# Top-k attention and a GELU MLP: the first batch's attention tile row by tile row, its MLP in chunks of 128 tokens

## The chip, the cores and the metric

The kernel runs on one core of a Trainium2 chip. The core has a matrix engine (PE, with PEld for its weight loads), a vector engine (DVE), an activation engine (ACT), a general engine (POOL), and queues that issue DMAs (SP's above all). The metric is the device time of one execution in microseconds (us), the median of several runs; lower is better.

## The reference

Inputs are q, k, v of 8 batches, 8 heads, 576 tokens, 64 columns, and two weight matrices, 512 x 2048 and 2048 x 512, which arrive in double precision.

```python
scores = scale * np.matmul(q, k.transpose(0, 1, 3, 2))
kth = np.partition(scores, -32, axis=-1)[..., -32:-31]
scores = np.where(scores >= kth, scores, -1000000000.0)
attn = np.exp(scores - np.max(scores, axis=-1, keepdims=True))
attn = attn / (np.sum(attn, axis=-1, keepdims=True) + 1e-09)
x = np.matmul(attn, v)                    # then (B,H,S,D) -> (B*S, H*D) = 4608 x 512
h = x @ w_in
g = 0.5 * h * (1.0 + erf(h / sqrt(2)))
return g @ w_out
```

## The kernel before

**Attention.** Heads are taken in pairs: 4 pairs a batch, 32 in all. An item is a pair and a tile of 128 query rows (`t` 0 to 3); the last 64 rows of two pairs make one item (`t` = 4). There are 18 items a batch, 144 in all, and the list `items` gives their order. One slot `n` of the main loop runs, for different items at once: `scores(n + 2)` (PE, copied to SBUF by ACT), the search `top_k(n)` on DVE, `threshold(n)` on POOL, the two `softmax(n - 1, e)` halves on ACT (they leave the unnormalised P and its row sum `den`), `add_small` (POOL) and `inverse` (DVE, `rden` = 1/den), `normalise(n - 1)` (POOL: P times `rden`, 128 x 1152), `transposes(n - 2)` (PE, copied to `pt` by ACT) and `attend(n - 3)` (PE: P times v for two tiles of a pair at once, 256 columns wide, copied to `xT` by ACT).

A search finds the 32nd largest of 576 scores by rounds of eight (MAX8, then MATCH_REPLACE8). A paired search works on lists of 288, the larger and the smaller of two halves (`larger` on DVE, `sum_up` and `smaller` on POOL); a single search (items below `PAIRED` = 2, and those in `SINGLE`, 18 to 27) works on all 576.

**Weights.** 16 units of two 128 x 512 blocks come as double-precision words and are turned to float32 in three steps (`weights_size`: two on ACT, the third on ACT or, for slots in `ON_DVE`, on DVE) and an addition on POOL (`weights_add`), one unit a slot from slot 1 on in `ORDER`. A unit's words are loaded two slots ahead into buffers that lie in weight arrays not yet filled.

**MLP.** x is kept transposed in `xT`. The tokens are cut in `units` of a token range and some of the 16 row blocks `f` of `w_in`; pairs of units make blocks of eight pieces. First-layer pieces (`l1_piece`) are products of `w_in` with 256 (or 128) tokens. GELUs run on ACT when a block is done. Second-layer pieces are plain for the first 256 tokens (`full_piece`, 512 wide) and, for the tokens after them, seven products in place of eight (`seven_piece`, `trio_piece`; they need POOL's `sums` of g and, made once in slots `sums_in`, `weight_sums` of `w_out`), or for a tail of 128 tokens `even_piece`. All blocks stand in one list `pieces`. `mlp(n)` runs the next n of them at places in the slot, within `room_in(slot)`: four in slots 10 and 11, then one block a slot, one piece more or less by turns. Nothing runs before the first 256 tokens of all four pairs are done, that is before slot 10 (`ready`). Until then `keep_busy` gives PE products of the identity.

PSUM has eight banks: two for scores and transposes (`pr`), two for first-layer blocks (`l1`), three for the second layer (`y0` to `y2`), and `z`. Small PE results (`bank`) turn through `z`, `y0`, `y1`, `y2` until `few` is set in slot 13, and then use `z` alone.

The order on each engine is the order in which the program issues; each engine waits in order.

## Time and profile before

| | us |
|---|---|
| median of 3 runs (1557.78 to 1558.49) | 1557.83 |
| the profiled execution, first to last instruction (its span) | 1553.6 |
| PE busy | 1524.1 |
| DVE busy | 1330.3 |
| ACT busy | 1166.7 |
| POOL busy | 1141.6 |
| start of slot 0 (first MAX8 of the search) | 10.29 |
| start of slot 30 | 316.84 |

The span stands for the execution's own time; the median is 4.2 us above it. Rows that name a line of the kernel give the engine, the operation, what it writes and reads, its shape and count; then the busy time in us, the mean length of one instruction in ns, and the idle time of the engine before them, with who ended it. An instruction's mean length contains what overlaps with the next one. Rows of stretches give the stretch, its length, and per engine the busy time and the number of instructions, then PE's granted clock, the DMA engines' busy share and GB/s. Rows of the timeline and the merged chain start with the time in us and the length.

### The profile page before, as it was taken

The numbers are of one execution on the slowest core, as the hardware profiler recorded it, in microseconds if no ns is written. First come the engines' busy times: TensorE is split into PE (matmuls) and PEld (weight loads), VectorE is DVE, ScalarE is ACT, GpSimd is POOL, SyncE is SP. The second block draws the span as 40 slices with busy tenths as digits, with TensorE's granted clock in tenths as the row PEclk, the third lists the DMA queues.
The fourth block names the chain that finished last, engine by engine and source line by source line (L and its number), as shares of the span: only waits on it lengthen the run. The fifth ranks groups of instructions, "written<-read, shape, count | busy, mean of one in ns | idle before, by whom it ended". The sixth has DMA issues, their size and how long they took to land.

```text
span 1553.6 us, 28121 instructions
## 1 busy us (share of the span) xinstructions
PE 1524.1 (98%) x9280; PEld 1199.8 (77%) x9280; DVE 1330.3 (86%) x4571; ACT 1166.7 (75%) x2050; POOL 1141.6 (73%) x1291
## 2 busy tenths in 40 slices
PE   8999999999999999999999999999999999999998
PEld 6776578877777778887777778788777777787887
DVE  7998799999989988898989998988998998998700
ACT  6998887777777787777777777777777777777720
POOL 4986657767787868777787877776788786876632
PEclk9999999999999999999999999999999999999999
DMA  6513210012101110012201111012110111000000
GB/s 176 164 67 128 70 45 1 1 41 50 24 15 31 38 28 27 1 30 45 40 15 18 28 31 45 1 24 36 32 24 22 24 30 32 15 1 15 7 14 14
DMA packets 185297, 56.35 MB, mean 36 GB/s; under 512 B 176160, under 2 KB 176704, under 8 KB 185152
## 3 DMA queue, kind: packets, MB, share of 16 engines
q1 hardware_dynamic: 183888, 54.13, 14.6%
q8 instruction: 73, 1.20, 0.3%
q14 instruction: 72, 0.59, 0.1%
q10 hardware_dynamic: 1200, 0.39, 0.1%
q0 software_dynamic: 64, 0.03, 0.0%
HBM read 45.08 MB, written 9.44 MB: 35 GB/s over the span
## 4 chain that ended last, share of the span: by engine, by line
PE 79%; POOL 6%; DVE 3%; ACT 1%; issue 1%; DVEq 0%; POOLq 0%
PE h_ps L668 29%; PE y_ps L806 17%; PE o L610 8%; PE tp L553 7%; PE s_ps L370 6%; PE seven L804 3%; POOL s L507 2%; PE y_ps L768 2%; PE y_ps L771 2%; PE tp_t L333 2%; PE o L621 1%; PE y_ps L750 1%; PE tp_t L527 1%; PE s_ps L385 1%; DVE top L450 1%; DVE lists L453 1%
## 5 line engine op out<-in xcount | busy, mean ns | idle before, releaser
L668 PE MATMUL h_ps<-xT,w_in_sb 128*128 128x256 f32 (+1 forms) x2560 | 542.7, 361 | 1.9 <-ACT xT L615 1.9
L668 PEld LDWEIGHTS h_ps<-xT,w_in_sb 128*128 128x128 f32 x2560 | 433.7, 191 | 72.6 <-issue 25.3
L450 DVE MAX8 top<-lists 128x8 f32<-128x288 f32 x792 | 321.2, 447 | 0.0
L507 POOL TENSOR_TENSOR s<-s,rden 128x1152 f32<-128x1152 f32 x144 | 302.7, 2102 | 0.3 <-DVE rden L482 0.3
L496 ACT ACTIVATE s<-s,bias 128x576 f32<-128x576 f32 x288 | 223.4, 776 | 11.9
L453 DVE MATCH_REPLACE8 lists<-top,lists 128x288 f32<-128x288 f32 x528 | 229.8, 443 | 0.0
L495 ACT ACTIVATE s<-s,neg 128x576 f32<-128x576 f32 x288 | 225.8, 784 | 2.9 <-POOL neg L475 2.7
L450 DVE MAX8 low<-lists 128x8 f32<-128x288 f32 x528 | 213.1, 446 | 0.0
L569 ACT COPY pt<-tp 128x1024 f32<-128x1024 f32 x133 | 135.1, 1016 | 102.0 <-PE tp L553 102.0
L488 POOL TENSOR_SCALAR den<-den 128x2 f32<-128x2 f32 x144 | 31.4, 218 | 233.4 <-ACT s L496 229.0
L421 POOL TENSOR_TENSOR lists<-lists 128x576 int32<-128x576 int32 x132 | 186.3, 1411 | 4.0
L413 POOL TENSOR_TENSOR lists<-s 128x576 int32<-128x576 int32 x132 | 185.6, 1406 | 0.0
L610 PE MATMUL o<-pt,raw_v 128*64 128x256 f32 x1280 | 153.4, 385 | 0.4 <-ACT pt L560 0.4
L610 PEld LDWEIGHTS o<-pt,raw_v 128*64 128x64 f32 x1280 | 86.6, 137 | 86.6 <-issue 44.1
L475 POOL TENSOR_SCALAR neg<-kth 128x2 f32<-128x2 f32 x132 | 85.7, 649 | 88.6 <-DVE kth L466 88.0
L553 PE MATMUL tp<-ident,s 128*128 128x128 f32 x1152 | 149.6, 273 | 0.0
L553 PEld LDWEIGHTS tp<-ident,s 128*128 128x128 f32 x1152 | 134.6, 141 | 14.8 <-issue 1.6
L806 PE MATMUL y_ps<-w_out_sb,sum 128*128 128x256 f32 x480 | 142.8, 379 | 0.0
L482 DVE RECIPROCAL rden<-den 128x2 f32<-128x2 f32 x144 | 23.3, 162 | 136.9 <-POOL den L488 136.2
L378 ACT ACTIVATE s<-s_ps 128x1024 f32<-128x1024 f32 x127 | 124.2, 1025 | 15.7 <-PE s_ps L370 15.4
L370 PE MATMUL s_ps<-kt,qm 64*128 64x512 f32 x512 | 131.4, 627 | 0.8 <-ACT s L376 0.8
L684 ACT ACTIVATE g<-h_ps 128x512 f32<-128x512 f32 x144 | 78.2, 595 | 49.9 <-PE h_ps L668 49.2
(148 smaller groups left out, 2826.4 us busy)
## 6 DMA issues: line engine op xcount, KB each, us to landing
raw_v<-in_v_dram SPq DMA_DIRECT2D x64, 128.0 KB, 2.3
out_dram<-y SPq DMA_DIRECT2D x30, 256.0 KB, 2.1
w_out_sb<-in_moe_w_in_dram SPq DMA_DIRECT2D x14, 511.8 KB, 4.9
raw_q<-in_q_dram SPq DMA_DIRECT2D x96, 64.0 KB, 2.0
raw_k<-in_k_dram SPq DMA_DIRECT2D x96, 64.0 KB, 2.0
w_out_sb<-in_moe_w_out_dram SPq DMA_DIRECT2D x10, 511.8 KB, 4.2
w_sum<-in_moe_w_out_dram SPq DMA_DIRECT2D x6, 511.8 KB, 4.0
raw_q<-in_q_dram SPq DMA_DIRECT2D x96, 8.0 KB, 1.8
```

Of the source, the lines that this page charges most:

```text
L370: nc.tensor.matmul(s_ps[:, e], lhsT=q_t[rows, :], rhs=kt[rows, 0:SM], start=True, stop=True)
L413: nc.gpsimd.tensor_tensor(t[:, 1].bitcast(i32), a.bitcast(i32), b.bitcast(i32), op=ALU.add)
L421: nc.gpsimd.tensor_tensor(both, both, top, op=ALU.subtract)
L450: nc.vector.max(x[:, e], src[:, e])
L453: nc.vector.match_replace(dst[:, e], x[:, e], src[:, e], LOWEST)
L495: nc.scalar.activation(s, s, func=AF.Prelu, bias=st["neg"][:, e : e + 1], scale=1.0, alpha=STEEP)
L496: nc.scalar.activation(s, s, func=AF.Exp, bias=st["bias"][:, e : e + 1], scale=1.0, accum_out=st["den"][:, e : e + 1],)
L507: nc.gpsimd.tensor_tensor(s, s, wide, op=ALU.mult)
L553: nc.tensor.transpose(tp[:, j * P : (j + 1) * P], s[:, first + j * P : first + (j + 1) * P], ident)
L610: nc.tensor.matmul(o[e * D : (e + 1) * D, 0:n], lhsT=vt[:, j, e, :], rhs=pt[:, e * NM + j if j < NM else 2 * NM, :], start=(j == 0), stop= ...
L668: nc.tensor.matmul(h_tile(u)[:, i, :], lhsT=w_in_sb[:, ko, f * P : (f + 1) * P], rhs=xT[:, ko, c0 : c0 + n], start=(ko == 0), stop=(ko == ...
L806: nc.tensor.matmul(acc[names][:, k], lhsT=lhsT, rhs=rhs, start=(j == 0 and k == 0), stop=(j == FT // 2 - 1 and k == 1),)
```

## The change

- The first batch's 16 whole-tile items come tile by tile and, within one, pair by pair: `items` for b = 0 is `(p, t)` with t outermost. After four items 128 tokens are done for all pairs. The raw q and k of all four pairs are loaded and transposed ahead, three pairs before slot 0, on three queues.
- These items run in `early_slot`: transposes in the slot of their softmax (`n - 1`), `attend(n - 2)` for one tile, 128 columns wide. P isn't normalised; two products with a broadcast `rden` put 1/den in the same bank, ACT copies the product to `xT`, and DVE multiplies it there, behind round 0 of the slot's search.
- The first 640 tokens of the MLP are plain; the first 512 of them in chunks of 128. Blocks of the first two chunks are interleaved; two first-layer blocks (`HELD`) stand in `y0`, `y1`. The MLP begins in slot 5, and from slot 12 to 29 its pieces are spread evenly; from slot 30 on a slot has the blocks that it had before.
- Units are converted in the order 0 to 15 in slots 1 to 16; the third step runs on DVE for slots 8 to 16. Single searches move to slots 31 to 39, `weight_sums` to 30 to 37.
- Small PE results turn through `z` and `y2` from slot 5 to 17.

```diff
@@ raw q and k
+    front = w_sum.rearrange("p a b n -> p (a b n)")
+    for y, region in enumerate((early, front[:, 0 : 2 * RAW], front[:, 2 * RAW : 4 * RAW])):
+        for x, n in enumerate("kq"):
+            raws[n].append(region[:, x * RAW : (x + 1) * RAW].rearrange("p (j e d) -> p j e d", j=NJ, e=2))
...
-    ORDER = [0, 1, 2, 3, 8, 9, 4, 5, 10, 11, 6, 7, 12, 13, 14, 15]
+    ORDER = list(range(UNITS))
     START = 2 * NP + 2
+    FIRST = NP + 1
+    EARLY = NP * NM
-    ON_DVE = range(START + 1, START + 9)
-    SINGLE = range(18, 28)
+    ON_DVE = range(8, UNITS + 1)
+    SINGLE = range(31, 40)
-    SLOT_OF = dict(zip(ORDER, [*range(1, START + 1), *range(START + 3, START + 9)]))
+    SLOT_OF = dict(zip(ORDER, range(1, UNITS + 1)))
...
         main = [
             (b * NP + p, tt + d) for tt in range(0, NM, 2) for p in range(NP) for d in range(2)
-        ]
+        ] if b else [(p, t) for t in range(NM) for p in range(NP)]
...
-        tag = "z" if few[0] else ("z", "y0", "y1", "y2")[turn[0] % 4]
+        tags = ("z",) if few[0] else ("z", "y2") if begun[0] else ("z", "y0", "y1", "y2")
+        tag = tags[turn[0] % len(tags)]
...
@@ top_k
             if r == len(rounds) - 1:
                 last()
+            if r == 0:
+                yield
@@ normalise
-        if i < 0 or i >= N:
+        if i < EARLY or i >= N:
             return
@@ transposes
+        if i < EARLY:
+            new_pt()
+            pr[0] = pair_tile("tp")
+            def ends():
+                nc.scalar.copy(
+                    out=pt_now[0][:, 0 : 2 * NM, x : x + P],
+                    in_=pr[0].rearrange("p e (j n) -> p (e j) n", j=NM),
+                )
+                tails(None)
+            return [lambda: turn_over(pr[0][:, 0], 0), lambda: turn_over(pr[0][:, 1], 1), ends]
@@ attend
-            copies.append(lambda: nc.scalar.copy(out=xT[:, at, c], in_=o[:, 0:n]))
+            if i < EARLY:
+                r = stat_of[i]["rden"]
+                for e in range(2):
+                    wide = bass.AP(
+                        tensor=r.tensor, offset=r[:, e : e + 1].offset, ap=[list(r.ap[0]), [0, D]]
+                    )
+                    nc.tensor.matmul(
+                        o[e * D : (e + 1) * D, P : 2 * P], lhsT=wide, rhs=ident, start=True, stop=True
+                    )
+                nc.scalar.copy(out=xT[:, at, c], in_=o[:, 0:P])
+                copies.append(lambda: nc.vector.tensor_tensor(
+                    xT[:, at, c], xT[:, at, c], o[:, P : 2 * P], op=ALU.mult
+                ))
...
@@ units
-        for tok, n in ((0, 256), (256, 256), (SM, 2 * TL), (COLS, 256), (COLS + 256, 256)):
+        whole = [(0, 256), (256, 256)] if base else [(t * P, P) for t in range(NM)]
+        for tok, n in (*whole, (SM, 2 * TL), (COLS, 256), (COLS + 256, 256)):
...
+    HELD = (2, 6)
...
-        return "even" if n < 256 else "full" if tok == 0 else None
+        return "full" if tok < COLS else "even" if n < 256 else None
...
-    blocks = [behind(first_block(0), 7, 0), behind(first_block(2), 7, 2)]
-    for u in range(2, NU, 2):
+    blocks = [behind(first_block(u), 7, u) if u in HELD else first_block(u) for u in (0, 2, 4, 6)]
+    blocks += [second_block(0), second_block(4), behind(first_block(8), 7, 8)]
+    blocks += [second_block(2), second_block(6), behind(first_block(10), 7, 10)]
+    for u in range(10, NU, 2):
         blocks.append(second_block(u - 2))
...
+    SPREAD = (12, 30)
     def room_in(n):
         x = n - START - 1
-        if x < 1:
-            return 4
+        if n < SPREAD[0]:
+            return min(7 if n < 9 else 6, sum(sizes[:4]) - done[0])
+        if n < SPREAD[1]:
+            ends = sum(sizes[:4]), sum(sizes[: SPREAD[1] - START - 1])
+            part = (n - SPREAD[0] + 1) / (SPREAD[1] - SPREAD[0])
+            return min(10, round(ends[0] + part * (ends[1] - ends[0])) - done[0])
         if x >= len(sizes):
             return 0
         return sizes[x] + (1 if x % 2 == 0 else -1)
...
-    load("k", 1)
+    load("k", 1, nc.scalar)
     load("q", 1)
-    for n in range(1, 3):
-        load_weights(n)
+    load("q", 2)
+    load("k", 2, nc.scalar)
+    load("k", 3, nc.gpsimd)
+    load_weights(1)
+    load("q", 3)
+    load("v", 0)
+    load_weights(2)
...
-    sums_in = {START + 8 + j: j for j in range(FT // 2)}
+    sums_in = {30 + j: j for j in range(FT // 2)}
+    def early_slot(n):
+        left[0] = room_in(n) if n >= FIRST else 0
+        begun[0] = n >= FIRST
+        if not waits(unit_in(n)):
+            weights_add(unit_in(n))
+        larger(n + 1)
+        scores(n + 2)
+        product = attend(n - 2)
+        searches = top_k(n, lambda: inverse(n - 1))
+        next(searches)
+        copy_x()
+        ready[0] = n_tok[0]
+        softmax(n - 1, 0)
+        mlp(1)
+        softmax(n - 1, 1)
+        if waits(unit_in(n)):
+            weights_size(unit_in(n))
+            weights_add(unit_in(n))
+        u = unit_in(n + 1)
+        whole = u is None or waits(u)
+        if not whole:
+            weights_size(u, 0)
+        mlp(2)
+        if n < FIRST:
+            keep_busy(6 if product else 12, ident)
+        prep = prep_in.pop(n, [])
+        for piece in prep[:1]:
+            piece(None)
+        tr = transposes(n - 1) if n - 1 < EARLY else []
+        for piece in tr:
+            piece()
+            mlp(1)
+        for piece in prep[1:]:
+            piece(None)
+            mlp(1)
+        if n < FIRST:
+            keep_busy(8, ident)
+        smaller(n + 1)
+        add_small(n - 1)
+        mlp(left[0])
+        if not whole:
+            weights_size(u, 1)
+        run_gelus()
+        for _ in searches:
+            pass
+        threshold(n)
+        normalise(n - 1)
+        sum_up(n + 2)
+        run_small(6)
+        next_loads(n)
+    LAST_EARLY = EARLY + 1
+    for n in range(LAST_EARLY + 1):
+        early_slot(n)
     ahead = N + 4
-    for n in range(ahead):
+    for n in range(LAST_EARLY + 1, ahead):
...
-        two = few[0] and n % 2 == 0 and n + 3 < N and items[n + 3][1] < NM
+        two = n % 2 == 0 and n + 3 < N and items[n + 3][1] < NM and not h_of
```

More of the change, by code (lines that the diff above doesn't have):

```diff
@@ L295, in piece @@
             ahead = 1 if pair >= SQUARES else 2
-            if pair + ahead > SQUARES and pair < SQUARES and pair % 2:
+            if pair < NP or pair + ahead > SQUARES and pair < SQUARES and pair % 2:
                 return
@@ L909, in first_block, with words_of @@
         need = units[u][0] + units[u][1]
-        return [(need, lambda w=w, x=x: l1_piece(w, x)) for w in (u, u + 1) for x in range(4)]
+        def words_of(w, x):
+            _, _, f0, nf = units[w]
+            c = 2 * ((f0 + x // (4 // nf)) * P // WS)
+            return (c, c + 1)
+        return [
+            (need, words_of(w, x), lambda w=w, x=x: l1_piece(w, x)) for w in (u, u + 1) for x in range(4)
+        ]
     def second_block(u):
@@ L955, in mlp @@
         for _ in range(n):
-            if done[0] >= len(pieces) or pieces[done[0]][0] > ready[0] or left[0] == 0:
+            if done[0] >= len(pieces) or pieces[done[0]][0] > ready[0] or left[0] <= 0:
                 return
-            pieces[done[0]][1]()
+            if not all(w in made for w in pieces[done[0]][1]):
+                return
+            pieces[done[0]][2]()
             done[0] += 1
@@ L992 @@
     keep_busy(WARM, idle)
-    for pair in range(2):
+    for pair in range(3):
         for piece in transpose_qk(pair, pair == 0):
             piece()
-        if pair == 0:
-            scores(0)
-            scores(1)
+        if pair < 2:
+            scores(pair)
     slots_of = [
@@ L1011 @@
     ]
-    first = {2: (0, 1, 1), 3: (2, 2, 3)}
+    first = {3: (0, 0, 0)}
     prep_in, squares_in = {}, {}
-    for pair in range(2, n_pairs):
+    for pair in range(3, n_pairs):
         b, p = divmod(pair, NP)
@@ L1089 @@
         ready[0] = n_tok[0]
-        if late:
-            softmax(n - 1, 1)
+        softmax(n - 1, 1)
         smaller(n + 1)
         add_small(n - 1)
-        for piece in tr[-1:] + prep:
+        for piece in prep[1:]:
             piece(None)
             mlp(1)
-        if n == 1:
-            keep_busy(8, ident)
         run_gelus()
@@ L1103 @@
         if n < N:
-            top_k(n, lambda: inverse(n - 1))
+            for _ in top_k(n, lambda: inverse(n - 1)):
+                pass
         else:
@@ L1112 @@
         run_small(6)
-        if not waits(unit_in(n + 1)):
-            weights_size(unit_in(n + 1))
-        for m in (n + 1, n + 2):
-            if m > 2 and waits(unit_in(m)) == (m == n + 1):
-                load_weights(m)
-        if n < NP:
-            load("v", n)
     ready[0], left[0] = NT, len(pieces)
```

138 lines of the change are left out of this document (72 added, 66 removed).

## The prediction

> **What bounds the kernel now.** I read the page first, then the busy time of each engine in stretches cut at the starts of attention slots, then single slots in the timeline, then the groups by form for prices.
>
> ```profile
> span 1553.6 us, 28121 instructions
> PE 1524.1 (98%) x9280; PEld 1199.8 (77%) x9280; DVE 1330.3 (86%) x4571; ACT 1166.7 (75%) x2050; POOL 1141.6 (73%) x1291
> PE   8999999999999999999999999999999999999998
> DVE  7998799999989988898989998988998998998700
> ```
>
> PE looks full from start to end. It isn't, as the prices of its groups show:
>
> ```profile
> L668 PE MATMUL h_ps<-xT,w_in_sb 128*128 128x256 f32 x2048 | 480.8, 382 | 1.9 <-ACT xT L615 1.9
> L610 PE MATMUL o<-pt,raw_v 128*64 128x256 f32 x1280 | 153.4, 385 | 0.4 <-ACT pt L560 0.4
> L668 PE MATMUL h_ps<-xT,w_in_sb 128*128 128x128 f32 x512 | 61.9, 277 | 0.0
> L990 PE MATMUL warm<-ident 128*128 128x128 f32 x366 | 46.6, 287 | 0.0
> L750 PE MATMUL y_ps<-w_out_sb,g 128*128 128x512 f32 x64 | 29.8, 592 | 0.0
> ...
> L668 PEld LDWEIGHTS h_ps<-xT,w_in_sb 128*128 128x128 f32 x2560 | 433.7, 191 | 72.6 <-issue 25.3
> ```
>
> L990, 46.6 us, multiplies the identity for nothing. All of it lies in the first ten slots, where the MLP has no input yet. The stretches below are slots 0 to 4, 5 to 10, 11 to 17, 18 to 29, 30 to 39, 40 to 143, and what follows the last search (columns: length, then busy time and instructions of PE, PEld, DVE, ACT, POOL, clock, DMA share, GB/s):
>
> ```profile
> 10.29:57.68 47.39, 39.11 (x244) 28.45 (x244) 47.28 (x139) 41.21 (x69) 31.41 (x28) 0.89 0.69 196
> 57.68:112.31 54.63, 52.61 (x411) 43.65 (x410) 53.12 (x193) 53.75 (x90) 49.31 (x43) 1.00 0.24 86
> 112.31:192.37 80.06, 77.47 (x407) 47.63 (x407) 64.25 (x230) 70.38 (x113) 51.54 (x46) 1.00 0.34 102
> 192.37:316.84 124.47, 123.94 (x854) 98.18 (x853) 118.39 (x280) 97.55 (x172) 86.40 (x116) 1.00 0.08 21
> 316.84:416.78 99.94, 98.97 (x548) 78.43 (x546) 92.93 (x331) 76.83 (x138) 71.64 (x79) 1.00 0.20 36
> 416.78:1470.90 1054.12, 1047.65 (x6432) 831.74 (x6429) 949.17 (x3387) 808.53 (x1438) 819.89 (x933) 1.00 0.12 24
> 1470.90:1553.60 82.70, 76.16 (x362) 65.18 (x360) 2.85 (x8) 15.97 (x34) 28.88 (x40) 0.98 0.04 13
> ```
>
> Call them A, B, C, D, E, F, G. In A and B the search on DVE sets the pace (47.28 of 47.39, 53.12 of 54.63). In C it is PE together with the softmax chain, in D PE and DVE together, from E on PE with DVE close behind. One slot's cost on DVE stands in the timeline, paired and single searches:
>
> ```profile
> 48.81 0.45 DVE L450 MAX8 first<-lists 128x8 f32<-128x288 f32 x1
> 57.68 0.46 DVE L450 MAX8 first<-lists 128x8 f32<-128x288 f32 x1
> ...
> 244.88 0.74 DVE L450 MAX8 first<-s 128x8 f32<-128x576 f32 x1
> 254.58 0.74 DVE L450 MAX8 first<-s 128x8 f32<-128x576 f32 x1
> ```
>
> A paired search takes 8.87 us a slot, a single one 9.70: 0.83 more.
>
> **The sum, stage by stage.** The list of MLP blocks has the same length from slot 30 on, so each slot there gets the same pieces as before. F and G I leave at their times. What changes is how long it takes to reach slot 30, and E. All terms are against the profiled execution of 1553.6 us, which lies 4.2 us below the median of 1557.83; I add the sum to the median.
>
> Prices of a piece, from the merged chain (16 wide, 32 narrow instructions, 24 of the seven-product blocks):
>
> ```profile
> 646.97 3.57 PE h_ps L668 x32
> ...
> 1474.27 3.46 PE h_ps L668 x16
> ...
> 1507.98 5.18 PE y_ps L806 x24
> ```
>
> A 256-wide instruction takes 0.216 us, a 128-wide one 0.112. A first-layer piece is 4 x 0.216 = 0.86 before and 8 x 0.112 = 0.89 after: 64 pieces of the first 512 tokens cost 1.9 us more in all. The Trainium skill, "TensorE: Matmul & The Clock Gate", section "Back-to-back issue gap", speaks against narrow chunks: in a stream with weight loads it gives about 81 ns a matmul at N=128 and 131 at N=512, far from proportional; halfway (an estimate, 98 ns at 256) a narrow pair would cost 1.65 times the wide one, and the 64 pieces about 36 us more instead of 1.9. The rows here, 3.57/32 against 3.46/16, disagree with it.
>
> A second-layer piece is two 512-wide instructions, 2 x 29.8/64 = 0.93 us. A seven-product block is 28 instructions of 0.216, 6.0 us; eight plain pieces are 7.4.
>
> A, slots 0 to 4. Three products of xT by the broadcast reciprocal enter DVE's queue, behind round 0 of the search, at slots 2 to 4. The rows next to it:
>
> ```profile
> L338 DVE TENSOR_SCALAR s<-t_ps 128x128 f32<-128x128 f32 x1 | 0.3, 291 | 1.0 <-PE t_ps L333 1.0
> L888 DVE TENSOR_TENSOR y<-y_ps,y 128x256 f32<-128x256 f32 x1 | 0.4, 425 | 70.6 <-PE y_ps L806 70.6
> L208 DVE TENSOR_SCALAR w_out_sb<-w_out_sb 128x1024 int32<-128x1024 uint32 x3 | 2.1, 692 | 0.0
> ```
>
> Same width, one operand fewer: 0.29; twice the width: 0.43. I take 0.29 (bounds 0.2 and 0.43), so 3 x 0.29 = +0.9. Ahead of the slots, ACT now issues eight more DMAs (pairs 1 and 2 of K), and nothing of SP's is moved later that slot 0 needs:
>
> ```profile
> 0.73 1.09 ACTq L116 DMA_DIRECT2D raw_k<-in_k_dram  x2
> ...
> 7.42 0.59 ACT L286 COPY qm<-tp_qk 128x512 f32<-128x512 f32 x1 [4.29 <-PE tp_qk L281]
> ```
>
> Eight at 0.55 are 4.4 us, under ACT's idle 4.29: nothing, or 2 us if those loads slow the first K and Q.
>
> B, slots 5 to 10. The MLP starts here: 28 pieces of 0.89 = 24.9 us. They take the place of warming: by its order of instructions the changed kernel keeps 164 of L990's 366, all in A, so 202 x 46.6/366 = 25.7 us go. PE, 52.61 of 54.63, is no fuller than it was. DVE gets six products (1.7) and the weights' third step in four slots (4 x 0.69 = 2.8): 53.12 + 4.5 = 57.6. ACT hands over that third step but takes the GELUs of two units in slot 8:
>
> ```profile
> L684 ACT ACT_TABLE_LOAD x68 | 87.2, 1283 | 1.1
> L684 ACT ACTIVATE g<-h_ps 128x512 f32<-128x512 f32 x144 | 78.2, 595 | 49.9 <-PE h_ps L668 49.2
> ```
>
> Two table loads and four GELUs: 2.6 + 2.4 = 5.0 us in one slot of an ACT that is busy 53.75 of 54.63. The next softmax and the product that DVE waits for stand behind it. I charge 0.9 above DVE's need: 58.5, +3.9 (from +3.0 to +8, where the whole 5.0 shows).
>
> C, slots 11 to 17. Rows of L668 alone, then of L750 alone, in C and D (PE's and PEld's busy time and counts):
>
> ```profile
> 112.31:192.37 80.06, 28.20 (x114) 19.96 (x112) 1.00 0.34 102
> 192.37:316.84 124.47, 45.77 (x256) 38.04 (x256) 1.00 0.08 21
> ...
> 112.31:192.37 80.06, 22.41 (x48) 8.61 (x48) 1.00 0.34 102
> 192.37:316.84 124.47, 7.36 (x16) 2.88 (x16) 1.00 0.08 21
> ```
>
> Before, C has 114 x 0.216 + 48 x 0.465 = 46.9 us of MLP. After: 44 pieces, 12 of the first and 32 of the second layer: 10.7 + 29.8 = 40.5. The broadcast of 1/den by two extra 64-column products, 4 instructions, in pairs side by side as L610's are, costs 2 x 153.4/1280 = 0.24 a slot, 1.7. PE: 6.4 - 1.7 = 4.7 less, 77.47 to 72.8. DVE's need goes from 64.25 to 65.6 (seven products, five weight steps for six). What stands between these and 80.06 is here:
>
> ```profile
> DVE rden L482 <- POOL den L488: 15.6, 7, 3.2
> ```
>
> DVE waited 15.6 us in C for den, that is for the second softmax half, which ACT ran late in the slot. Now both halves stand ahead of the slot's MLP pieces, and POOL drops the division of P. I take 74, -6 (from -7.3, PE's 72.8, to 0).
>
> POOL's division goes with 16 of these:
>
> ```profile
> L507 POOL TENSOR_TENSOR s<-s,rden 128x1152 f32<-128x1152 f32 x144 | 302.7, 2102 | 0.3 <-DVE rden L482 0.3
> ...
> 34.76 2.40 POOL L227 TENSOR_TENSOR w_in_sb<-w_in_sb,w_out_sb 128x1024 int32<-128x1024 int32 x1
> ```
>
> 16 x 2.10 = 33.6 us of POOL, worth nothing by itself (49.31 of 54.63 busy in B), but the addition that frees a weight buffer ended at 37.16, 6.1 us into slot 2, and ends 2.1 earlier without it:
>
> ```profile
> 31.05 0.45 DVE L450 MAX8 first<-lists 128x8 f32<-128x288 f32 x1
> ...
> w_out_sb<-in_moe_w_in_dram SPq DMA_DIRECT2D x14, 511.8 KB, 4.9
> ```
>
> That matters because DVE now takes the next weights behind round 0 of the following search, a fifth of the slot in (some 1.8 us, an estimate from 8.87), no more at its end. The words land 6.1 - 2.1 + 4.9 = 8.9 us after the slot's start, the second load half a microsecond later, and are wanted at 8.87 + 1.8 = 10.7: under 2 us of cover. If it fails, the whole search waits behind this step; SP's order has only loads of Q and K ahead of them.
>
> D, slots 18 to 29. MLP before: of the 256 L668 two blocks, 128 instructions, are narrow (the 128 tail tokens); with 16 of L750, four seven-product blocks and an even one (112 + 32 instructions of 0.216) it is 27.6 + 14.3 + 7.4 + 31.1 = 80.4 us. After: 40 + 40 pieces, 35.7 + 37.2 = 72.9; PE 7.5 less, 116.4. All ten single searches leave: DVE 118.39 - 10 x 0.83 = 110.1. POOL takes paired steps back and loses the weight sums; at 86.40 of 124.47 it hides either. Between 110.1 and 117 I take 113, since both engines fall together: -11.5.
>
> E, slots 30 to 39. Nine single searches and the weight sums arrive: DVE 92.93 + 9 x 0.83 = 100.4 of a stage of 99.94. At least +0.5, at most 9 x 0.83 = +7.5; the slots alternate between PE and DVE, so I take +4.5.
>
> Sum: 0.9 + 3.9 - 6 - 11.5 + 4.5 = -8.2 us. 1557.83 - 8.2 = **1549.6 us**. With all lower ends (0.6 + 3.0 - 7.3 - 14.4 + 0.5 = -17.6) it is 1540.2; with all upper ones (3.3 + 8 + 0 - 7.5 + 7.5 = +11.3) 1569.
>
> **Rivals.** *Slower, a new wait on DVE.* The product with 1/den waits for PE's product with v and ACT's copy of the same slot, and behind it stand all further rounds of the search, the threshold, and so the next softmax. In C a wait of the same sort cost 15.6/7 = 2.2 us a slot. At that price in all 13 slots 5 to 17 it is 28.6 us, of which B and C as forecast already hold 9.3 above DVE's need (0.9 and 8.4): +19.3, **1569**. It decides from (8.2 + 9.3)/13 = 1.35 us a slot. For it: ACT's full row in B, its lump in slot 8, and that short PE results now turn through two PSUM banks, not four, one of them held until this product is done. Against: the forecast's C has a shorter softmax chain, and the product comes a fifth of a slot late. 0.21.
>
> *Deeper gain.* Each stage reaches the need of its fullest engine: -17.6, **1540**. For it: four engines evenly loaded. Against: F ran 1054.12 where DVE needed 949.17 and the seven-product blocks were priced without a stall. 0.17.
>
> *Nothing left.* PE keeps its stalls: only PE's own 4.7 and 7.5 leave, and E takes 7: -12.2 + 0.9 + 3.9 + 7 = -0.4, **1557**. 0.12.
>
> *Narrow chunks cost their weight loads.* If the mean 191 ns of L668's LDWEIGHTS showed instead of 112, 64 pieces x 8 x 0.079 = +40, **1590**. The 3.57-us row speaks against; this is what the skill's section above would point to. 0.02.
>
> That the pieces are not spread as said I leave at nothing: in the changed kernel's order of instructions all 152 of the pieces stand ahead of slot 30.
>
> **How the numbers follow.** Forecast 0.48, deeper 0.17, nothing left 0.12, new wait 0.21, weight loads 0.02. A change of 0.2% (3.1 us) is about what measurement can tell. Faster: 0.48 + 0.17 = 0.65; same 0.12; slower 0.23. The range, 1538 to 1566, holds nearly all of the bounds' sums, the deeper gain and all but the far end of the new wait.
>
> **What would show it.** Slot 5 should start near 58.6 us, slot 11 near 117, 18 near 191, 30 near 304, 40 near 408, with the last 103 slots in 1054. L990 on the identity should be down to 164 instructions and some 21 us, none after slot 4. The product's wait on DVE should stay under 1 us a slot. I am wrong if slot 30 starts later than 312, if DVE's waits in slots 5 to 17 pass 15 us, if E lengthens by over 7.5, or if narrow L668 costs over 0.13 an instruction.

## The result, and the profile after

The changed kernel takes 1605.02 us (1604.71 to 1606.28) against 1557.8 us: 1.0311 times as long [1.0296, 1.0325]. The forecast was 1549.6 us, its range 1538 to 1566. The profiled execution has a span of 1603.1 us, 49.5 us more than before.

The page of the changed kernel (whole span; engine, busy time, share, instructions; then tenths in 40 slices):

```profile
span 1603.1 us, 28504 instructions
PE 1519.8 (95%) x9478; PEld 1185.6 (74%) x9478; DVE 1346.1 (84%) x4605; ACT 1158.9 (72%) x2030; POOL 1096.8 (68%) x1253
PE   4878978899999999999999999999999999999998
DVE  3997978699999998988998998889998998888700
```

PE is busy for slightly less time than before (1519.8 against 1524.1 us). The time was lost in holes, nearly all of them in the first nine slices of 40 us. The same stages as in the prediction, cut at the starts of slots 0, 5, 11, 18, 30, 40 and at the end of the last search:

```profile
28.06:77.87 49.81, 42.46 (x356) 33.73 (x355) 47.93 (x143) 45.41 (x74) 25.29 (x25) 1.00 0.24 77
77.87:146.19 68.32, 55.82 (x472) 47.35 (x470) 61.39 (x203) 56.51 (x90) 38.14 (x37) 0.93 0.33 101
146.19:234.31 88.12, 72.39 (x484) 44.42 (x480) 73.00 (x237) 63.22 (x106) 42.47 (x42) 0.94 0.25 79
234.31:362.68 128.37, 117.85 (x822) 81.13 (x822) 107.03 (x387) 89.16 (x155) 70.70 (x75) 0.96 0.07 18
362.68:466.11 103.43, 101.40 (x547) 76.54 (x544) 101.83 (x233) 77.75 (x138) 65.45 (x91) 1.00 0.19 35
466.11:1520.00 1053.89, 1045.90 (x6413) 830.50 (x6413) 949.13 (x3387) 808.29 (x1435) 820.59 (x933) 1.00 0.12 24
```

| us | before | forecast | after | difference |
|---|---|---|---|---|
| start to slot 0 | 10.29 | 10.3 to 12.3 | 28.06 | +17.8 |
| A, slots 0 to 4 | 47.39 | 48.3 | 49.81 | +2.4 |
| B, slots 5 to 10 | 54.63 | 58.5 | 68.32 | +13.7 |
| C, slots 11 to 17 | 80.06 | 74 | 88.12 | +8.1 |
| D, slots 18 to 29 | 124.47 | 113 | 128.37 | +3.9 |
| E, slots 30 to 39 | 99.94 | 104.4 | 103.43 | +3.5 |
| F, slots 40 to 143 | 1054.12 | 1054.12 | 1053.89 | -0.2 |

Each early stage has an event of its own. From here on "DVE's step" is the third weight step, "the words" what it reads. The timeline before slot 0, at DVE's step in slot 8 beside POOL's addition, and at a PE stop in slot 22 (start, length, instruction, and in brackets the idle time before it and who ended it):

```profile
19.72 4.18 PE L1074 MATMUL warm<-raw_v 128*128 128x128 f32 x18 [19.72 <-DMA raw_v<-in_v_dram]
...
110.63 2.38 POOL L234 TENSOR_TENSOR w_in_sb<-w_in_sb,w_out_sb 128x1024 int32<-128x1024 int32 x1
110.76 2.81 DVE L215 TENSOR_SCALAR w_out_sb<-w_out_sb 128x1024 int32<-128x1024 uint32 x1
112.97 1.85 POOL L434 TENSOR_TENSOR lists<-lists 128x576 int32<-128x576 int32 x1
...
275.21 3.78 PE L383 MATMUL s_ps<-kt,qm 64*128 64x512 f32 x8 [4.21 <-ACT g L741]
```

The groups of DVE's step and of what waited, slots 5 to 17 (engine, line, waited for: us, times, longest):

```profile
L215 DVE TENSOR_SCALAR w_out_sb<-w_out_sb x6: 689/1872/2846, 99.4 to 173.0; 128x1024 int32<-128x1024 uint32 x6
L215 DVE TENSOR_SCALAR w_sum<-w_sum x3: 696/2837/2858, 161.2 to 212.1; 128x1024 int32<-128x1024 uint32 x3
DVE xT L657 <- ACT xT L656: 12.3, 6, 5.1
DVE w_sum L215 <- DMA w_sum<-in_moe_w_out_dram: 5.8, 1, 5.8
DVE w_out_sb L215 <- DMA w_out_sb<-in_moe_w_out_dram: 3.5, 1, 3.5
```

The first two rows give the least, median and greatest length in ns; six of the nine steps overlap POOL's addition and are 11.0 us longer in all than 0.69 each. So four suspects stand in the trace: the start, DVE's step (0.69 us where it is alone, 2.8 us beside POOL's addition), the words that come late, and the product with 1/den (L657). A fifth is PE's stop for GELUs.

### The profile page after: what moved, and what is told of

The parts are those of the page before. It is cut to its first block, busy times and chain, and to the rows that moved or that the text cites. A ratio compares the mean times of both kernels' runs of the same rounds, so it can differ in the third digit from the quotient of the medians.

```text
span 1603.1 us, 28504 instructions
## 1 busy us (share of the span) xinstructions
PE 1519.8 (95%) x9478; PEld 1185.6 (74%) x9478; DVE 1346.1 (84%) x4605; ACT 1158.9 (72%) x2030; POOL 1096.8 (68%) x1253
## 4 chain that ended last, share of the span: by engine, by line
PE 70%; DVE 9%; POOL 6%; ACT 2%; issue 2%; DMA 1%; SPq 1%; DVEq 0%; POOLq 0%; ACTq 0%
PE h_ps L721 25%; PE y_ps L862 14%; PE o L642 7%; PE tp L572 6%; PE s_ps L383 6%; DVE top L463 3%; PE y_ps L806 3%; PE seven L860 2%; POOL s L522 2%; DVE rest L466 2%; DVE lists L466 2%; PE tp_t L346 1%; PE y_ps L824 1%; PE y_ps L827 1%; PE o L667 1%
## 5 line engine op out<-in xcount | busy, mean ns | idle before, releaser
L721 PE MATMUL h_ps<-xT,w_in_sb 128*128 128x256 f32 (+1 forms) x2688 | 530.5, 348 | 3.5 <-DVE xT L657 2.0
L463 DVE MAX8 top<-lists 128x8 f32<-128x288 f32 x798 | 325.3, 452 | 0.0
L522 POOL TENSOR_TENSOR s<-s,rden 128x1152 f32<-128x1152 f32 x128 | 269.3, 2104 | 0.3 <-DVE rden L497 0.3
L511 ACT ACTIVATE s<-s,bias 128x576 f32<-128x576 f32 x288 | 223.8, 777 | 12.3 <-issue 0.4
L588 ACT COPY pt<-tp 128x1024 f32<-128x1024 f32 x128 | 130.1, 1017 | 103.6 <-PE tp L572 103.6
L434 POOL TENSOR_TENSOR lists<-lists 128x576 int32<-128x576 int32 x133 | 190.5, 1433 | 4.4
L572 PE MATMUL tp<-ident,s 128*128 128x128 f32 x1152 | 153.4, 274 | 10.3 <-ACT s L511 10.3
L642 PEld LDWEIGHTS o<-pt,raw_v 128*64 128x64 f32 x1440 | 92.8, 137 | 87.9 <-issue 48.1
L642 PE MATMUL o<-pt,raw_v 128*64 128x256 f32 (+1 forms) x1440 | 154.8, 361 | 0.0
L862 PE MATMUL y_ps<-w_out_sb,sum 128*128 128x256 f32 x448 | 133.2, 379 | 0.0
L466 DVE MATCH_REPLACE8 lists<-low,lists 128x288 f32<-128x288 f32 x266 | 116.9, 451 | 0.0
```

What stands on the lines that cost most here:

```text
L434: nc.gpsimd.tensor_tensor(both, both, top, op=ALU.subtract)
L463: nc.vector.max(x[:, e], src[:, e])
L466: nc.vector.match_replace(dst[:, e], x[:, e], src[:, e], LOWEST)
L511: nc.scalar.activation(s, s, func=AF.Exp, bias=st["bias"][:, e : e + 1], scale=1.0, accum_out=st["den"][:, e : e + 1],)
L522: nc.gpsimd.tensor_tensor(s, s, wide, op=ALU.mult)
L572: nc.tensor.transpose(tp[:, j * P : (j + 1) * P], s[:, first + j * P : first + (j + 1) * P], ident)
```

## The experiments

Ratios are against the kernel before, on the same chip. Where two changed kernels are compared, what one has more or less than the other is the difference of their ratios times 1557 us.

**1. The warm-up waits for v.** `keep_busy(WARM, idle)` multiplies the last tile of `raws["v"][0]`, and the change put `load("v", 0)` ahead of it. Undone:

```diff
-    load("v", 0)
-    load_weights(2)
     keep_busy(WARM, idle)
+    load("v", 0)
+    load_weights(2)
```

> Only the load of v's first pair (and the second weight unit behind it) is issued after the warming products instead of ahead of them. Theory: the warming products read the tail block of the buffer that this load fills, so PE's whole queue waits for it, and slot 0 starts at 28.06 instead of 10.29 us. Then slot 0 starts near 10.5 us and the kernel takes 1605 - 17.6 = 1587.5 us. Rival: the eight extra early loads of q and k set the start (the first k and q land late). Then slot 0 starts at 14 to 18 us and the time is 1591 to 1596.

1593.27 us, 1.0227 [1.0212, 1.0242], 13.1 us less than the changed kernel: slot 0 starts at 15.07 instead of 28.06. That is inside the rival's 14 to 18 us and short of the theory's 10.5: the wait of the warm-up makes 13.0 us of the late start, and 4.8 us have another cause. The reverse, the kernel before with `load("v", 0)` put ahead of its warm-up:

> The kernel before, with the load of v's first pair issued ahead of the warming products instead of at the end of slot 0. Theory: the warming products read that buffer's tail block, so PE's queue waits for the load, which stands behind the loads of q, k and two weight units; slot 0 starts at 17 to 22 us instead of 10.3 and the time is 1565 to 1570 us. Rival: the late start of the changed kernel came from its other early loads; then this one starts within 1 us of 10.3 and the time is 1558 us.

1568.49 us, 1.0076 [1.0059, 1.0093]. Its timeline shows the whole effect, slot 0 at 25.17 for 10.29:

```profile
17.51 3.67 PE L990 MATMUL warm<-raw_v 128*128 128x128 f32 x18 [17.51 <-DMA raw_v<-in_v_dram]
25.17 1.42 DVE L450 MAX8 first<-s 128x8 f32<-128x576 f32 x2 [1.41 <-ACT s L375]
```

One line's place is worth 14.9 us of start; the end moves by 11 to 12. The rest of the late start is in the timeline of the run with the warm-up free:

```profile
8.25 0.38 ACTq L118 DMA_DIRECT2D w_sum<-in_k_dram  x1
9.07 0.55 ACTq L121 DMA_DIRECT2D w_sum<-in_k_dram  x1
9.65 1.28 ACT L299 ACT_TABLE_LOAD   x1 [9.65 <-DMA w_sum<-in_k_dram]
10.95 0.59 ACT L299 COPY qm<-tp_qk 128x512 f32<-128x512 f32 x1
```

The eight added loads that ACT issues do not end near 6.3 us, eight times 0.55 after their start at 1.85; their issues are spread until 9.6, and the first copy of `qm`, at 7.42 before, comes at 10.95.

**2. DVE's step moved behind the search.** The third step of slots 7 to 14 is issued after the slot's search, as in the kernel before, not before round 1 of it; `third(u)` is the instruction taken out.

```diff
@@ weights_size
         if on_dve(u):
-            nc.vector.tensor_scalar(
-                w.bitcast(i32), w.bitcast(u32), 2.0**-13, None, op0=ALU.mult
-            )
+            if part is None:
+                third(u)
@@ early_slot
         for _ in searches:
             pass
+        if not whole:
+            third(u)
```

> Only DVE's third weight step of slots 7 to 14 moves from behind round 0 of the search to behind its last reduction. Theory: in mid-slot it meets POOL's additions and lasts 1.35 to 2.86 us in place of 0.69, and once waits 3.5 us for the words; 10.9 + 3.5 us leave DVE's queue in slots 7 to 14, and the time is 1605 - 10 to 14 = 1591 to 1595 us, the step 0.69 us in each slot. Rival: DVE isn't what those slots wait for (PE and ACT are as full), so the time falls by under 4 us, to 1601 or more.

1597.63 us, 1.0257 [1.0241, 1.0272]: 8.4 us less. All nine steps are short:

```profile
L223 DVE TENSOR_SCALAR w_out_sb<-w_out_sb x6: 684/687/687, 105.8 to 173.7; 128x1024 int32<-128x1024 uint32 x6
L223 DVE TENSOR_SCALAR w_sum<-w_sum x3: 684/694/696, 162.8 to 204.7; 128x1024 int32<-128x1024 uint32 x3
```

In the profiled executions DVE is busy for 10.6 us less in B and C, and the two stages are 7.2 us shorter: most of the step's extra length had been time on the path. The theory had asked for a little more, 10 us or over.

**3. No paired scores before slot 30.** Two items' scores at once put the second in the bank of the first-layer blocks, where PE has to wait for GELUs.

```diff
-        two = n % 2 == 0 and ...
+        two = n >= 30 and n % 2 == 0 and ...
```

> Only the scores of slots 18 to 29 are no more made two at a time (the second one no more goes to the bank pair of the first MLP layer). Theory: with pieces spread evenly a GELU can stand behind the slot's second softmax half when these scores come, so PE stops in slots 22 and 24 (16.0 and 15.5 us) and its clock halves. Then no slot of 18 to 29 passes 12 us and the time is 1605 - 10 to 13 = 1592 to 1595 us. Rival: the slots are long because PE has too many pieces left; the wait moves to the first-layer pieces behind that GELU and the time falls by under 4 us.

1594.92 us, 1.0237 [1.0222, 1.0253], 11.5 us less. In the profile only D is shorter, by 10.6 us; here slots 11 to 17 and 18 to 29:

```profile
147.09:236.02 88.93, 74.43 (x472) 45.27 (x471) 73.82 (x237) 62.98 (x104) 42.34 (x42) 0.90 0.24 77
236.02:353.83 117.81, 114.94 (x821) 79.13 (x821) 107.00 (x387) 88.65 (x155) 70.68 (x75) 1.00 0.08 20
```

**4. All three.** The edits of 1, 2 and 3 together.

> All three edits. Theory: three separate waits, at different places, so the gains add: 17.6 + 12 + 11.5 = 41, 1564 us, still above the kernel before by what DVE's product waits (13 us in slots 2 to 17) and the late words of slot 16 (5.8 us) cost. Rival: the new rhythm of slots 5 to 17 itself is bound by the chain PE, ACT, DVE in each slot; then taking the weight step away only uncovers the wait for the product, and the time stays over 1572 us.

1572.77 us, 1.0093 [1.0076, 1.0109]: 33.9 us less, where the three alone make 13.1 + 8.4 + 11.5 = 33.0. Three separate losses, then, that do not hide each other. The rival's bound of 1572 was just passed as well: DVE's wait for the product grew from 12.3 to 18.5 us in slots 5 to 17.

**5. The product with 1/den two rounds later** (`if r == 0: yield` to `r == 2` in the search), on experiment 4's kernel. This edit stays in all runs that follow.

> The three edits of before, and DVE's product with 1/den moved from behind round 0 to behind round 2 of the slot's search (some 3 us later in DVE's queue). Theory: with the three edits DVE still waits 21 us in slots 2 to 17 for ACT's copy that this product needs (3.4 us in slots 9 and 12, 4.7 in 17); three more rounds of search ahead of it hide 12 to 18 us of them, and the time falls from 1572.8 to 1555 to 1561 us. Rival: the slot's chain through PE and ACT is as long as the slot, so DVE meets the same wait at the end of the search (for den) and the time falls by under 5 us.

1572.8 us, 1.0099 [1.0084, 1.0115]: nothing. The product's waits in slots 5 to 17 fall from 18.5 to 10.7 us, but 6.6 us of waits for den take their place:

```profile
DVE xT L663 <- ACT xT L662: 10.7, 7, 2.5
DVE rden L503 <- POOL den L509: 6.6, 7, 2.9
```

DVE needs `rden` once a slot, and den is the last thing that ACT's softmax yields. Where ACT is late, DVE waits at one place or the other.

**6. ACT's queue free at the start:** k of pair 1 on SP's queue, of pair 2 on POOL's.

```diff
-    load("k", 1, nc.scalar)
+    load("k", 1)
-    load("k", 2, nc.scalar)
+    load("k", 2, nc.gpsimd)
```

> As the run above, and the first loads of k for pairs 1 and 2 issued by SP and POOL instead of ACT. Theory: eight issues hold ACT until 9.1 us and its table load until 10.9, so its first copy comes 4 us late; slot 0 then starts near 10.5 instead of 15 us and 4.3 to 4.6 us are gained. Rival: the DMA engines, not ACT's queue, are what is full in the first 10 us (share over 1); pair 0's data or pair 1's come later and under 2 us are gained.

1567.43 us, 1.0066 [1.0051, 1.0081], 5.1 us less: slot 0 at 9.73, the start wholly regained. ACT's table load is back at 1.85 us, as in the kernel before.

**7 and 8. The last unit.** Unit 15's words go where unit 14's lay, which the addition one slot before sets free, and are turned and added within slot 16. In that slot of the run just told:

```profile
181.12 0.84 SPq L192 DMA_DIRECT2D w_sum<-in_moe_w_out_dram  x2
186.46 1.26 ACT L210 ACTIVATE w_sum<-w_sum,high 128x1024 f32<-128x1024 int16 x1 [1.57 <-DMA w_sum<-in_moe_w_out_dram]
186.47 0.69 DVE L223 TENSOR_SCALAR w_sum<-w_sum 128x1024 int32<-128x1024 uint32 x1 [5.72 <-DMA w_sum<-in_moe_w_out_dram]
189.04 2.37 POOL L240 TENSOR_TENSOR w_out_sb<-w_out_sb,w_sum 128x1024 int32<-128x1024 int32 x1 [13.62 <-DVE lists L472]
173.73:194.15 20.42, 12.48 (x71) 6.53 (x70) 9.84 (x36) 12.52 (x19) 6.13 (x7) 0.80 0.33 78
```

First its third step was put on ACT (`ON_DVE = range(8, UNITS)`):

> As the run above, and the third step of weight unit 15 on ACT instead of DVE. Theory: in slot 16 DVE waits 5.5 us for the words of that unit, whose buffer is freed only by the addition of unit 14 in the slot before; with that step on ACT, DVE goes on, and 3 to 6 us are gained. Rival: ACT then waits for the same words in slot 16 and holds the softmax and the copy for slot 17, so the time is the same within 2 us.

1567.95 us, 1.0071 [1.0056, 1.0086]: nothing. ACT then stands at the words itself, and DVE waits 9.7 us for den. Then, from experiment 6's kernel again, the unit came one slot later, like the others: its load is the last of slot 15 in SP's order, its steps stand at the usual places of slot 16 and its addition in slot 17:

```diff
-    ON_DVE = range(8, UNITS + 1)
+    ON_DVE = range(8, UNITS + 2)
-    SLOT_OF = dict(zip(ORDER, range(1, UNITS + 1)))
+    SLOT_OF = dict(zip(ORDER, [*range(1, UNITS), UNITS + 1]))
     def waits(u):
-        return u == ORDER[-1]
+        return False
```

> The kernel with ACT's queue free, unit 15 one slot later: its words are loaded after slot 15 into the buffer that unit 14's addition left in that slot, turned in slot 16, added in slot 17, like every other unit. Theory (slot 16 is long because the words arrive inside it, and DVE, ACT and the softmax stand behind them): slot 16 falls from 20.4 us to about 12, a few pieces that need unit 15 move to slot 17 and make it 0 to 2 us longer; 1567.4 - 6 to 8, about 1560 (1558 to 1563). Rival (slot 16 is long because PE and ACT are behind by then anyway, and the words only end last): slots 16 and 17 together stay above 29 us (31.96 now), 1565 or more.

1562.58 us, 1.0034 [1.0022, 1.0047], 5 us less; slot 16 falls to 14.92 us, not to 12, and DVE's wait for words to 0.6. The words still come late, for SP issues their load at 179.94, 7.4 us into slot 16, behind 8.8 us of issues of q and k; but DVE now meets them after its search. Its waits in slots 5 to 17, and its step in slot 16:

```profile
DVE xT L663 <- ACT xT L662: 9.0, 7, 2.3
DVE rden L503 <- POOL den L509: 5.1, 7, 1.5
DVE w_sum L223 <- DMA w_sum<-in_moe_w_out_dram: 0.6, 1, 0.6
...
185.14 1.77 DVE L223 TENSOR_SCALAR w_sum<-w_sum 128x1024 int32<-128x1024 uint32 x1 [0.60 <-DMA w_sum<-in_moe_w_out_dram]
```

This kernel, called the mended one below, is the base of all that follow. Its stages A to E, then slots 9, 12 and 13:

```profile
9.52:57.45 47.93, 39.85 (x330) 32.02 (x330) 47.82 (x143) 42.76 (x69) 25.39 (x25) 1.00 0.58 165
57.45:120.23 62.78, 53.86 (x471) 45.33 (x470) 56.88 (x203) 56.57 (x93) 38.81 (x38) 0.95 0.37 113
120.23:197.32 77.09, 68.96 (x493) 44.48 (x492) 67.81 (x237) 63.63 (x107) 41.87 (x41) 0.96 0.30 89
197.32:320.52 123.20, 120.33 (x838) 81.44 (x838) 107.01 (x387) 89.70 (x156) 70.62 (x75) 1.00 0.08 22
320.52:423.95 103.43, 101.41 (x547) 76.54 (x544) 101.84 (x232) 77.68 (x138) 65.36 (x91) 1.00 0.19 35
97.05:110.58 13.53, 9.95 (x88) 8.14 (x87) 9.75 (x36) 13.25 (x21) 6.58 (x7) 1.00 0.22 79
129.89:143.03 13.14, 9.49 (x53) 5.02 (x54) 9.74 (x35) 13.00 (x21) 6.57 (x7) 1.00 0.23 82
143.03:152.69 9.66, 9.66 (x56) 5.49 (x55) 9.63 (x35) 8.29 (x15) 6.61 (x7) 1.00 0.07 16
```

B is still 8.2 us longer than before. In slots 9 and 12 ACT is the full engine; in the other slots from 5 to 17 but slot 16 it is DVE or PE, or both, as in slot 13.

**9. GELUs of the first four blocks each when its block is done**, not two blocks at once (all four blocks `behind`, no `gelus(u - 2)`).

> As the run with unit 15 later, and GELUs of the first four blocks run each when its block is done, not two blocks at once. Theory (two table loads and four GELUs in one slot make slots 9 and 12 13.0 us each, where their neighbours take 9.7 to 10): the two slots fall to about 10.5 each, the two extra table loads' 2.6 us lie in slots 6 and 10 and cost at most 2 of it; 2 to 4 us less than with unit 15 later alone, about 1557. Rival (ACT's whole work counts there, not its lump: it is busy 7.6 to 9.5 us of every slot from 5 to 12): slots 6 and 10 grow by what 9 and 12 lose, and the 5 us of extra table loads show: the same or up to 4 us more.

1564.26 us, 1.0052 [1.0038, 1.0065]: 2.8 us more, the rival's side. Slots 9 and 12 fall to 12.6 and 11.9 us, but slots 7 and 11, 9.7 us each in the mended kernel, go to 13.1 and 11.6. The run has four table loads more, 5.1 us of ACT, and the four slots together take 3.2 us more: the lump was spread, but what it costs to spread it was more than that gained.

**10 and 11. The price of the single searches in E.** On experiment 9's kernel, none of slots 31 to 39 is single (`SINGLE = ()`):

> As the run with GELUs apart, and no search from slot 31 to 39 is single. Theory (slots 30 to 39 are longer than before by the nine single searches on DVE, 9 x 0.83 us, less what PE needed anyway): the stage falls from 103.4 to about 99.9, as before the change, 3.5 us less than with the GELUs apart. Rival (the single searches are there because POOL's weight sums and paired steps don't fit side by side: 9.75 to 10 us of POOL in its fullest slots already): POOL becomes the bound of slots 30 to 37, and the stage stays at 103 or grows to 106.

1570.74 us, 1.0090 [1.0076, 1.0103]: 5.9 us more. Slots 30 to 39, then slot 34 alone:

```profile
324.93:434.38 109.45, 102.22 (x536) 77.02 (x536) 92.93 (x331) 77.91 (x136) 93.03 (x109) 0.98 0.18 33
366.27:379.51 13.24, 13.04 (x69) 10.78 (x65) 9.62 (x34) 8.11 (x15) 12.25 (x17) 1.00 0.10 23
```

DVE falls to 92.93, but POOL has weight sums and paired steps at once, 12.25 of slot 34's 13.24 us, and DVE waits in the stage for what POOL yields late:

```profile
DVE rden L503 <- POOL den L509: 16.2, 6, 3.6
```

Half of them single, on the mended kernel, with at most 8 pieces a slot in D:

```diff
-    SINGLE = range(31, 40)
+    SINGLE = range(31, 40, 2)
-            return min(10, round(
+            return min(8, round(
```

> As the run with unit 15 later, with two edits in different stages. In slots 18 to 29 a slot takes at most 8 pieces of the MLP, not 10: slot 18 alone is 14.0 us there, all of it PE. Theory (a slot lasts as long as its fuller engine, so unevenness costs): the stage falls from 123.2 to about 121; rival (PE is the bound of the whole stage): it stays. In slots 31 to 39 every second search is single, not all: theory (DVE's nine dear searches are the price there, and POOL has room for half the paired steps): 103.4 to about 101; rival (POOL's lists come late as they did without any single search): 103.4 or more. Theories together 1558 to 1560, rivals together 1562 to 1565.

1561.9 us, 1.0031 [1.0020, 1.0042]: the same as the mended kernel. E is 104.10 for 103.43, D 122.35 for 123.20: both rivals. None of the three mixtures of single and paired searches made E shorter than 103.43. No run took the weight sums out of E, so what its 3.5 us consist of is not shown.

**12 to 14. The moved division, the GELUs' table loads, and both.** The mended kernel without the first 16 items' division (no broadcast products, no product on DVE); with copies in place of the GELUs of the first 256 tokens, which need no table load; and with both left out.

> As the run with unit 15 later, but the first 16 items are left undivided: no broadcast products, no product with 1/den on DVE. Theory (the moved division is what DVE pays in slots 2 to 17): DVE loses 16 products of 0.28 us and 9 us of waits for ACT's copy in slots 5 to 17; 5 to 10 us less than with unit 15 later, 1553 to 1558. Rival (the waits only change their place, as when the product was put later: ACT is late in those slots whatever DVE waits for): 0 to 4 us less, 1559 to 1563.

> As the run with unit 15 later, but the blocks of the first 256 tokens whose GELUs run in slots 9 and 12 are copied without GELU, which needs no table load: four ACT instructions each stay, two table loads each go. Theory (the lump of table loads and GELUs makes these slots 13.5 and 13.1 us): each loses 2.6 us, and the two together end near 21.5; 4 to 6 us less, about 1557.5. Rival (they are long because ACT's own row of the slot is full with weight steps and softmax): under 2 us less, 1561 or more.

> Both left out. If ACT is the one bound behind both, the gains overlap: more than the larger of the two single ones but 2 us or more short of their sum. If the two are separate prices, the gains add up.

| | us | ratio | against the mended kernel |
|---|---|---|---|
| without the division | 1558.6 | 1.0009 [1.0000, 1.0019] | -3.9 |
| copies for those GELUs | 1557.19 | 1.0000 [0.9992, 1.0009] | -5.3 |
| neither | 1553.26 | 0.9968 [0.9955, 0.9980] | -10.3 |

Without the division DVE's waits change their name. In slots 5 to 17, 15.9 us of them are for den, against 9.0 + 5.1 + 0.6 in the mended kernel:

```profile
DVE rden L503 <- POOL den L509: 15.9, 8, 4.1
```

So its 3.9 us are close to the instructions themselves (16 x 0.28 = 4.5), as the rival said: the waits only changed their place. With copies, two table loads go from each of slots 9 and 12, which are 2.7 and 2.5 us shorter, as the theory said:

```profile
97.12:107.93 10.81, 8.70 (x81) 7.38 (x80) 9.74 (x35) 10.46 (x19) 6.59 (x7) 1.00 0.28 99
129.03:139.66 10.63, 10.21 (x51) 5.84 (x52) 9.74 (x36) 10.52 (x19) 5.09 (x5) 0.84 0.27 101
```

Slot 9 is the clear case. In the copies' profile slot 11 is 1.8 us longer than in the mended kernel (ACT waits 2.0 us there for weight words, 0.9 in the mended kernel), so that C as a whole is 77.03 for 77.09, and what slot 12 gained does not show in the stage.

Together they give 10.3 where the parts make 9.2: two prices, added up, not one bound behind both. Even with its division and the four blocks' table loads for nothing, the arrangement with the big losses mended is only 5 us faster than the kernel before. No kernel that does all the work beat it.

## Why the prediction was wrong

**Start, the largest miss (forecast 0 to 2, measured 17.8).** The step that failed is "nothing of SP's is moved later that slot 0 needs". It looked at which loads come when, and not at what the warm-up reads. Experiment 1 and its reverse put that at 13 to 15 us of start. The rest was priced in the prediction as "nothing, or 2 us": eight issues at 0.55, hidden under ACT's idle 4.29. The row's price did not hold with three queues issuing: the eight took 7.3 us from the first to the end of the last (7.8 in experiment 1), and experiment 6, which took them off ACT, gave 5.1.

**A (+0.9; measured +2.4, and +0.5 in the mended kernel).** The products were 0.28 each for a forecast 0.29; the rest of the 2.4 is one wait of 1.8 us for ACT's copy.

**B (+3.9; measured +13.7).** The steps that failed are terms of the sum. DVE's step was charged 4 x 0.69 from a row where no addition of POOL's ran beside it; beside POOL's 2.4-us addition it is up to 2.86, and experiment 2 gave 8.4 us for it over B and C together. This could have been foreseen: the Trainium skill, "SBUF — State Buffer", section "Who interferes with whom", says that a tensor_scalar can run in a mode that takes the port pair that DVE shares with GpSimd, and that whichever engine issues first keeps it for its whole instruction. The rows agree: the step from 110.76 ends at 113.57, 0.56 us after POOL's 110.63 + 2.38, and POOL's next instruction, which began beside this rest, took 1.85 us, 1.40 in slot 9, where no step ran beside it. The prediction named the new place of the step, but only for its words. ACT's lump was charged 0.9 us above DVE's need, of at most 5.0, which would have made B +8; it came in slot 9 (the prediction had slot 8), and a second one in slot 12, which the sum for C does not hold. After the mending B stands at 62.78, +8.2, just past that upper end. In slot 9 ACT is busy for 13.25 of 13.53 us, so its two table loads are paid in full (experiment 13); without them and without the division B is 57.00 (experiment 14), so these two make 5.8 of the 8.2.

On those loads, the Trainium skill, "ScalarE: Activation LUTs", section "What ACT_TABLE_LOAD costs", gives about 2.66 us for a switch, 1.28 of load and 1.38 of drain. The two switches taken out of slot 9 gave 2.72 together, and 3.11 where the division was left out as well (13.02 to 9.91): 1.4 to 1.6 us a switch, little more than the 1.28 of the load, so most of that drain does not show here.

**C (-6; measured +8.1).** "Under 2 us of cover" for the words, with the whole search behind them, was the right place and priced at nothing. DVE waited 3.5 us there in slot 11: the addition freed the buffer at 138.43, but SP issued the load only at 146.09, behind eight loads of q and k that it issued from 140.43 on, which the prediction names and gives no time. The other wait, 5.8 us in slot 16, is unit 15's, whose load is issued in the slot that uses it, and which the prediction did not price; slot 16 took 20.4 us in the run of experiment 6. DVE's step beside POOL's addition is in C as well, with 6.5 of the 11.0 us.

**D (-11.5; measured +3.9).** Two faults. The paired scores behind GELUs in slots 22 and 24, which the prediction did not look for, took 10.6 us: without them D is 117.81, -6.7. And 113 was never open: the prediction had itself 116.4 for PE alone and took a value between that and DVE's 110.1, though a stage cannot be shorter than its fullest engine's work.

**C and D after the mending.** The two have to be read together, because they are cut at DVE's searches and work that PE does not get done in C falls into D: C is 77.09 (-3.0) and D 123.20 (-1.3), 200.29 us against 204.53 before and a forecast of 187. PE's busy time is 189.29, close to the prediction's 72.8 + 116.4 = 189.2, so the 187 was less than PE alone needs. The work left PE as foreseen; the time did not follow, since PE, idle for 3.1 us in the two stages before, is idle for 11.0 in the mended kernel. That is most of what still separates the mended kernel from the forecast: its slot 40 starts 15.4 us later than the sum says, 13.3 of it in C and D and 4.3 in B.

**E (+4.5; measured +3.5), F and G** held, with DVE busy for 101.83 us in E for a forecast 100.4, and so did the prices of PE's work. The groups of the changed kernel:

```profile
L721 PE MATMUL h_ps<-xT,w_in_sb 128*128 128x128 f32 x896 | 112.3, 279 | 3.4 <-DVE xT L657 2.0 <-ACT g L741 1.1 <-ACT s L391 0.3
L1074 PE MATMUL warm<-ident 128*128 128x128 f32 x164 | 20.5, 278 | 0.0
L657 DVE TENSOR_TENSOR xT<-xT,o 128x128 f32<-128x128 f32 x16 | 4.5, 283 | 14.1 <-ACT xT L656 14.1
```

Narrow products cost 112.3 / 896 = 0.125 us (0.121 before, counted the same way), and 0.128 with the 128 that fill `y0` and `y1`. That is under the bound of 0.13, so chunks of 128 are not what made it slow, and the rival of weight loads fell. The warming is down to the 164 instructions foreseen, in 20.5 us.

**The rivals.** "A new wait on DVE" named a wait that came, 12.3 us in slots 5 to 17, 0.95 a slot and under its point of 1.35; with the three losses of experiment 4 gone it was 18.5, 1.42 a slot and over it. But its price of 19.3 us was wrong: putting the wait elsewhere or taking the product away (5, 12) turned it into a wait for den, and without the product only 3.9 us were gained. No single engine bounds those slots in the mended kernel: ACT does in 9 and 12, DVE or PE in the others but 16. Two of the prediction's signs of being wrong came: slot 30 started at 362.68, later than 312, and DVE's waits in slots 5 to 17 were 21.6 us, over 15. The time was lost by four events that no rival held: the warm-up, DVE's step beside POOL's addition, the late words, the paired scores. With ACT's queue as a fifth the experiments took back 13.1, 8.4, 5.0, 11.5 and 5.1 us, 43 of the 48 that the ratio of 1.0311 makes.

Open stays what the granted clock cost (0.93 and 0.94 in B and C, 0.95 and 0.96 mended, 1.00 before): no run held PE busy there with all else the same. Slot 16 of the mended kernel still takes 14.92 us. Its trace has DVE waiting 1.92 us for the product's copy, 1.45 for den and 0.60 for words, and the step 1.08 us longer than alone, beside POOL's work on lists; without these 5.05 us it would be 9.87. No run took them out. What keeps PE idle in the mended kernel's C was not tried either.

## What to carry to other kernels

When a load is moved, look for everything that reads its buffer, also what reads it only to have something to do. A duration from a row holds for what ran beside it there: before an instruction of DVE or a queue's issue is priced at a new place, look who is busy at that place. And a stage's forecast is bounded below by the work of its fullest engine; a wait seen on one engine may only change its name when its cause is moved: take the work out altogether to learn its price.

## What was not expected of the hardware

One DVE instruction of 128 x 1024, 0.69 us alone, took 2.8 us whenever POOL's 2.4-us addition had begun 0.12 to 0.13 us before it (four steps), 2.39 where it came 0.57 us after the addition's start and 1.35 where it came 1.61 after: it was not slowed in proportion, but ended 0.56 to 0.59 us after the addition's end, in all six steps that met it. POOL's addition itself stayed at 2.4 us.

Two stops of PE for 4.2 us each in D were followed by about half the granted clock: 0.50 over the eight products of scores behind the one in slot 22 (275.20 to 278.90) and 0.62 behind the one in slot 24 (299.80 to 303.00). Around the first, with the end of the stop and what came after:

```profile
273.00:280.50 7.50, 5.29 (x44) 2.75 (x46) 7.36 (x28) 4.20 (x5) 5.72 (x6) 0.54 0.00 1
```

ACT's DMA issues, 0.4 to 0.8 us each in the rows, came up to 2 us apart while two or three queues were issuing the first loads, so that eight of them held ACT until 9.6 us.
